# Narrower attention products, a first cumulation of 256 gates, and one operation for the normalisation's small steps

## The chip, the cores and the metric

The kernel runs on one core of a Trainium2 chip. The metric is the device time of one execution in microseconds (us); lower is better. Engines are named as in the profile: PE (TensorE, its weight loads apart as PEld), DVE (VectorE), ACT (ScalarE), POOL (GpSimd), SP (SyncE, which here issues the DMAs).

## The reference

Causal attention with a gate, then two gated feed-forward layers, all in float32. Four batches of eight heads, 576 tokens, head dimension 64; model width 512, hidden width 1536, 2304 tokens.

```python
cum = cumsum(maximum(s, 0), axis=-1)                    # s: 4 x 8 x 576
bias = -(cum[..., :, None] - cum[..., None, :])
scores = where(causal, -1e9, q @ k.T / 8 + minimum(bias, 0))
attn = exp(scores - max(scores)); attn /= sum(attn) + 1e-9
x = (attn @ v)  -> 2304 x 512
xn = x / sqrt(mean(x * x) + 1e-6) * rms_g
x1 = (silu(xn @ w_gate) * (xn @ w_val)) @ w_out
out = (silu(x1 @ w2_gate) * (x1 @ w2_val)) @ w2_out
```

## The kernel before

Every large product is made of three: each operand is split into a high part (type float32r) and a low rest, and high x high, high x low and low x high are summed in PSUM. The instructions are not written in the order in which they run. Each step is recorded with an engine, a planned cost in ns, what it reads and writes, and a priority; `Plan.run` then plays a list schedule and emits every engine's instructions in that fixed order. A step recorded as one operation is emitted in one piece, whatever number of instructions it holds. On the chip each engine works through its list in order and waits where an operand is missing.

**Attention.** Queries are cut into tiles of 128 (the last has 64); group A is tiles 0 and 1 (256 queries), group B tiles 2 to 4 (320). The first 16 units, group A of batches 0 and 1, are *early units* (`EarlyUnit`): true float32 products, loads of 256 keys only. In such a unit the scores of tiles 0 and 1 are products of 128 and 256 columns (L716). The gate's cumulated sum enters as one more row of the contraction: a DMA (L705) copies 256 cumulated gates of this head from `cum` into row 64 of the operand `lq`. DVE adds the mask and takes the least (L601), ACT the exponent with its sum (L612), PE transposes (L726), DVE or ACT copies (L731, L732), PE multiplies by the values (L736), and the result goes to `x` (L741, L742). `cum` itself is made in `setup` by three DVE operations on all 32 heads x 576 gates: clamp (L473), scan (L476), shift and scale (L481).

The other units (`Unit`) take the split form. Group A there appears in batches 2 and 3 only: 16 units. Scores L575: for tile 0, 128 keys are wanted but `max(kl, 256)` columns are multiplied. Values L655: `pT` holds the transposed exponents; windows are padded with zero columns which `clear_pT` writes once, so that key block 1 of group A runs over 256 columns of which 128 are zero, and key block 3 of group B (32 units) over 256 of which 64 are zero. Its last window has 64 columns. Each window is two products, one for each part of `pT`.

**Normalisation** (`normalise`, 8 of them: groups A and B of four batches). ACT squares, PE sums (L767), and then 20 small DVE steps on a tile of 128 x 2 or 3 find each token's factor (L795 to L829). Each is an operation of its own, planned at 70 ns. PE transposes and spreads the factors (L833, L840), DVE multiplies (L844), and the parts of `x` are made (L847, L849).

**First layer's gate and value** (`moe1`, L860): 12 slices of the hidden width, for each group 24 products of 256 or 320 columns a slice. They need the normalised group and that slice's weights. Weights come by DMA (L382) and are converted by ACT, DVE and POOL (L384 to L400). Products of `moe1` have a low priority: PE takes them where attention leaves it free. The output product (L1019) and the second layer follow when attention is over.

Of the kernel before, what the change touches and what calls it, by code (L numbers as in the profile page):

```python
# [9 lines left out]
F32 = mybir.dt.float32  # L10
# [212 lines left out]
def c_mm(n):  # L223
    return 0.4167 * n + 13.3
# [26 lines left out]
TINY = 70  # L251


@with_exitstack
def tile_kernel(
# [87 lines left out]
    pT = {"A": [buf("at", f"pTA{i}", [P, 512], F32R) for i in range(2)],  # L343
# [76 lines left out]

    mask = buf("at", "ft", [P, 2 * P], F32, "mask")

    def setup():
# [44 lines left out]
        def clear_scores(en):  # L468
# [4 lines left out]
        op(DVE, 400, lambda en: en.tensor_scalar(  # L473
            out=cum(), in0=cum(), scalar1=0.0, scalar2=None, op0=ALU.max),
           r=[cum], w=[cum], pri=-1e6)
        op(DVE, 670, lambda en: en.tensor_tensor_scan(  # L476
            cum2(), cum(), cum(), 0.0, op0=ALU.add, op1=ALU.max),
           r=[cum], w=[cum2], pri=-1e6)


        op(DVE, 400, lambda en: en.tensor_scalar(  # L481
            out=cum(), in0=cum2(), scalar1=cum2()[:, S // 2:S // 2 + 1], scalar2=1.0 / SCALE,
            op0=ALU.subtract, op1=ALU.mult), r=[cum2], w=[cum], pri=-1e6)
        op(SP, 4 * NB * NH * S, lambda en: en.dma_start(out=cum_d, in_=cum()),
           r=[cum], w=["cum_d"], pri=-1e6)
# [61 lines left out]
    class Unit:  # L547
# [15 lines left out]
        def scores(self, pri):  # L563
# [53 lines left out]
        def values(self, pri):  # L617
            hd, g, nq = self.head, self.g, self.nq
            j = hd.j
            if g == "A":  # L620
                chunks = [([(1, 1), (0, 0), (0, 1)], [(0, 128, 384, P)])]
                wins = [(0, 256, 256, 0, P, (0,)), (1, 0, 256, 0, P, (0,))]
            else:
# [7 lines left out]
                        (2, 960, 320, 0, P, (1, 2)), (3, 0, 256, 64, P, (0,)),  # L631
# [36 lines left out]
    early_p = [buf("at", f"pTA{i}", [P, 512], F32) for i in range(2)]  # L668
    early_v = [buf("at", f"vl{i}", [P, 5, D], F32) for i in range(2)]

    class EarlyUnit(Unit):
# [6 lines left out]
        def __init__(self, b, h, x, tot):  # L678
# [8 lines left out]
            self.parts = lq_parts(early_q[i % 2], i // 2 % 2)  # L687
            self.vl = early_v[i % 2], i // 2 % 2
# [10 lines left out]
        def load(self, pri):  # L699
# [11 lines left out]
        def scores(self, pri):  # L711
            for t in self.tiles:
# [5 lines left out]
                    start=True, stop=True), r=[*self.parts, "lower rows"], w=[pt], pri=pri)  # L718
# [423 lines left out]
```

## Time and profile before

| | us |
|---|---|
| median of 3 runs | 1151.41 (1149.88 to 1152.21) |
| profiled execution, its own time | 1150.37 |
| its span | 1148.4 |
| PE busy | 1119.2 |
| DVE busy | 607.3 |
| ACT busy | 545.7 |

The span is the time from the first to the last instruction of the profiled execution; 2 us of its own time lie around it. PE is busy for 97% of it, but its busy time counts each product to its modelled end, so a product that follows another closely overlaps it; what a product costs in a row of products is read from the distance of starts. A true float32 product counts as two instructions in the trace. DVE and ACT are busy mostly in the first 300 us, in which attention runs.

### The profile page before, as it was taken

What the parts mean: (1) busy time and instruction counts of PE and PEld (TensorE: products, weight loads), DVE (VectorE), ACT (ScalarE), POOL (GpSimd) and SP (SyncE); (2) the same over time, 40 slices, a digit from 0 to 9 for tenths busy, and PEclk for the clock granted to TensorE, in tenths of its full rate; (3) what the DMA queues carried; (4) which work ended last, traced back from release to release, by engine and by line L of the source; (5) the groups of instructions that cost most, each with busy time, mean ns of one, the idle gap of its engine ahead of it and who ended that gap; (6) DMA issues with size and microseconds to landing.
All of it is one profiled execution on the core that took longest, in us unless ns stands there. A gap on an engine that the chain in (4) does not pass through costs nothing.

```text
span 1148.4 us, 18814 instructions
## 1 busy us (share of the span) xinstructions
PE 1119.2 (97%) x6708; PEld 1001.1 (87%) x6708; DVE 607.3 (53%) x1672; ACT 545.7 (48%) x1203; POOL 188.9 (16%) x282
## 2 busy tenths in 40 slices
PE   5889999999999999999999999999999999999998
PEld 3589999899999999999888788888888888888898
DVE  5898899979735875542686424432222222222222
ACT  5886889889434854431697435432111211211121
POOL 3343455354211300000021000001000100100000
PEclk9899999999999999999999999999999999999999
DMA  4874455334321223338756634211000100100000
GB/s 147 249 239 123 143 142 156 116 104 116 87 72 49 74 89 112 116 119 267 231 163 197 208 122 123 74 37 49 25 1 1 65 1 1 46 1 1 1 37 20
DMA packets 70221, 112.54 MB, mean 98 GB/s; under 512 B 11696, under 2 KB 39344, under 8 KB 70128
## 3 DMA queue, kind: packets, MB, share of 16 engines
q1 hardware_dynamic: 70128, 111.35, 31.6%
q8 instruction: 53, 0.87, 0.3%
q14 instruction: 40, 0.33, 0.1%
HBM read 87.63 MB, written 23.67 MB: 97 GB/s over the span
## 4 chain that ended last, share of the span: by engine, by line
PE 89%; DMA 3%; DVE 3%; ACT 2%; issue 1%; SPq 1%; POOL 0%; DVEq 0%; ACTq 0%
PE mo L860 50%; PE sps L1019 8%; PE tp L1019 8%; PE mo L1019 6%; PE sps L575 4%; PE tp L639 4%; PE tp L655 4%; DMA cvs<-in_w_gv 1%; PE mo L767 1%; PE tp L736 1%; PE sps L716 1%; DVE sc L601 1%; DMA hh<-h_d 1%; DMA lq<-cum 1%; PE tp L726 0%
## 5 line engine op out<-in xcount | busy, mean ns | idle before, releaser
L860 PE MATMUL mo<-xH,H 128*128 128x320 f32 (+1 forms) x768 | 228.1, 298 | 0.1
L860 PE MATMUL mo<-xL,H 128*128 128x320 f32 (+1 forms) x768 | 227.1, 296 | 0.5 <-POOL xL L849 0.5
L860 PE MATMUL mo<-xH,L 128*128 128x320 f32 (+1 forms) x768 | 227.0, 296 | 0.0
L869 DVE SCALAR_TENSOR_TENSOR t<-t,mo 128x256 f32<-128x256 f32 (+2 forms) x156 | 81.3, 521 | 257.7 <-ACT t L867 257.3
L867 ACT ACTIVATE t<-mo 128x256 f32<-128x256 f32 (+2 forms) x156 | 72.2, 463 | 284.8 <-PE mo L860 284.4
L860 PE MATMUL mo<-x1H,L 128*128 128x512 f32 (+1 forms) x480 | 176.6, 368 | 0.0
L860 PE MATMUL mo<-x1H,H 128*128 128x512 f32 (+1 forms) x480 | 176.6, 368 | 0.0
L860 PE MATMUL mo<-x1L,H 128*128 128x512 f32 (+1 forms) x480 | 176.6, 368 | 0.0
L1008 ACT ACTIVATE hH<-hh 128x512 fp32r<-128x512 f32 (+1 forms) x120 | 69.8, 585 | 169.4 <-DVE hh L872 133.1
L860 PEld LDWEIGHTS mo<-xL,H 128*128 128x128 f32 x768 | 144.2, 188 | 1.5 <-POOL xL L849 0.7
L860 PEld LDWEIGHTS mo<-xH,H 128*128 128x128 f32 x768 | 144.1, 188 | 1.0 <-issue 0.3
L860 PEld LDWEIGHTS mo<-xH,L 128*128 128x128 f32 x768 | 144.2, 188 | 0.4
L872 DVE TENSOR_TENSOR hh<-t,mo 128x256 f32<-128x256 f32 (+2 forms) x156 | 81.3, 521 | 99.4 <-PE mo L860 98.1
L1010 DVE TENSOR_TENSOR hL<-hh,hH 128x512 fp32r<-128x512 f32 (+1 forms) x120 | 79.6, 664 | 90.7 <-ACT hH L1008 90.3
L860 PEld LDWEIGHTS mo<-x1L,H 128*128 128x128 f32 x480 | 90.5, 189 | 15.0
L860 PEld LDWEIGHTS mo<-x1H,L 128*128 128x128 f32 x480 | 90.5, 189 | 14.9
L860 PEld LDWEIGHTS mo<-x1H,H 128*128 128x128 f32 x480 | 90.5, 189 | 14.7
L612 ACT ACTIVATE sc<-sc,col 128x512 f32<-128x512 f32 (+4 forms) x160 | 95.6, 598 | 15.6 <-DVE col L601 15.1
L1051 POOL TENSOR_TENSOR x1L<-x1l,x1H 128x512 fp32r<-128x512 f32 (+1 forms) x20 | 25.0, 1260 | 391.5 <-ACT x1H L1049 222.0
L639 PE MATMUL tp<-ident,sc 128*128 128x128 f32 x432 | 69.0, 278 | 1.3 <-DVE x L664 1.1
L1019 PE MATMUL sps<-hL,oH 128*128 128x512 f32 (+1 forms) x192 | 69.6, 364 | 0.1
L1019 PE MATMUL tp<-hL,oH 128*128 128x512 f32 (+1 forms) x192 | 69.4, 363 | 0.0
(129 smaller groups left out, 2097.0 us busy)
## 6 DMA issues: line engine op xcount, KB each, us to landing
raw<-in_w_gv SPq DMA_DIRECT2D x40, 512.0 KB, 4.8
cvs<-in_w_o SPq DMA_DIRECT2D x24, 512.0 KB, 3.7
hh<-h_d SPq DMA_DIRECT2D x48, 256.0 KB, 2.9
cb<-cum_d SPq DMA_DIRECT2D x32, 288.0 KB, 3.4
lq<-in_qk SPq DMA_DIRECT2D x32, 288.0 KB, 3.0
h_d<-hh SPq DMA_DIRECT2D x72, 128.0 KB, 2.2
vl<-in_vp SPq DMA_DIRECT2D x32, 160.0 KB, 3.1
cvs<-in_w_gv SPq DMA_DIRECT2D x8, 512.0 KB, 4.0
```

The costliest lines, as they stand in the source:

```text
L575: op(PE, c_mm(n), lambda en, pt=pt, o=o, c=c, n=n, z=z, kk=kk: en.matmul(pt()[:, :n], qst[j]()[:, o:o + 128], kk()[:, c:c + n], start=z == ...
L612: op(ACT, c_act(o + m, 2) + 35, lambda en: en.activation(sc()[:m, :o + m], sc()[:m, :o + m], ACTF.Exp, scale=-1.0, bias=col()[:m, 0, t:t + 1],
L639: op(PE, C_TR, lambda en, pt=pt, a=a, m=m, kb=kb, t=t: en.transpose(pt()[:, a:a + P], self.sc[t]()[:, kb * P:kb * P + P], ident()), r=[sel ...
L655: op(PE, c_mm(n), lambda en, w=w, z=z, kb=kb, d0=d0, n=n, o=o, kn=kn: en.matmul(po()[:, o:o + n], vst[j]()[:kn, kb, :], pT[g][z]()[:kn, d0 ...
L860: op(PE, c_mm(n), lambda en, a=a, x=x, c=c, k=k, i=i: en.matmul(ps()[:, :n], a()[:, c], x()[:, k, :n], start=(k == 0 and i == 0), stop=(k ...
L867: op(ACT, c_act(n), lambda en: en.activation(t()[:, :n], gp()[:, :n], ACTF.Tanh, scale=0.5), r=[gp], w=[t], pri=pri)
L869: op(DVE, c_tt(n), lambda en: en.scalar_tensor_tensor(out=t()[:, :n], in0=t()[:, :n], scalar=1.0, in1=gp()[:, :n], op0=ALU.add, op1=ALU.mu ...
L872: op(DVE, c_tt(n), lambda en: en.tensor_tensor(out=hh()[:, :n], in0=t()[:, :n], in1=vp_()[:, :n], op=ALU.mult), r=[vp_, t], w=[hh], pri=pri)
L1008: op(ACT, c_act(n) + 35, lambda en: en.activation(H()[:, :n], hh()[:, :n], ACTF.Copy), r=[hh], w=[H], pri=pri)
L1010: op(DVE, c_tt(n), lambda en: en.tensor_tensor(out=L()[:, :n], in0=hh()[:, :n], in1=f32(H()[:, :n]), op=ALU.subtract), r=[hh, H], w=[L], p ...
L1019: op(PE, c_mm(n), lambda en, d=d, c=c, w=w, x=x, i=i: en.matmul(acc_[d]()[:, :n], Wo[w]()[:, c], HL[x]()[:, :n], start=(f == 0 and i == 0) ...
L1051: op(POOL, c_ptt(n), lambda en, k=k, x=x: en.tensor_tensor(out=L()[:, k, :n], in0=x()[:, :n], in1=f32(H()[:, k, :n]), op=ALU.subtract), r= ...
```

## The change

- **Columns.** Scores of tile 0 in group A take 128 columns and not 256; key block 1 of group A takes 128 and not 256, key block 3 of group B 192 and not 256. `clear_pT` goes. The planner's cost of a product, `c_mm`, gets a least value of 72 ns.
- **First group's gates.** `cumulate` makes first a cumulation of 256 gates alone (`cumA`) and then the one of all 576. POOL clears the unused rows of `cumA` first. The first four early units (`FIRST = 4`) don't wait for a DMA of their gates: a second float32 product for each tile adds them, with one column of the identity, spread over 128, as the weights. The other early units copy from `cumA`.
- **Normalisation.** The sum's inverse is one operation of two instructions; the other 18 steps are recorded as one operation, planned at 170 ns each, without the planner's note that it shares a port with POOL.
- **Priorities of weights.** Conversions of `w_gv` come two units later, their loads at 8 + 1.0 f and not 6 + 1.5 f.

```diff
 def c_mm(n):
-    return 0.4167 * n + 13.3
+    return max(72.0, 0.4167 * n + 13.3)
+FIRST = 4
...
+        def clear_cum(en):
+            en.memset(cumA()[NB * NH:64], 0.0)
+            en.memset(cumA()[64:], 0.0)
+        op(POOL, 500, clear_cum, w=[(cumA, 1)], pri=-2e6)
...
+        def cumulate(out, n, pri):
+            rows = NB * NH
+            def steps(en):
+                en.tensor_scalar(out=cum()[:, :n], in0=cum()[:, :n], scalar1=0.0, scalar2=None,
+                                 op0=ALU.max)
+                en.tensor_tensor_scan(cum2()[:, :n], cum()[:, :n], cum()[:, :n], 0.0,
+                                      op0=ALU.add, op1=ALU.max)
+                en.tensor_scalar(out=out()[:rows, :n], in0=cum2()[:, :n],
+                                 scalar1=cum2()[:, n // 2:n // 2 + 1],
+                                 scalar2=1.0 / SCALE, op0=ALU.subtract, op1=ALU.mult)
+            op(DVE, 400 + 3.6 * n, steps, r=[cum], w=[cum, cum2, (out, 0)] if out is not cum
+               else [cum, cum2], pri=pri)
+        cumulate(cumA, 2 * P, -1e6)
+        cumulate(cum, S, -900)
...
-                parts = [(0, max(kl, 256))] if kl <= 512 else [(0, 288), (288, 288)]
+                parts = [(0, kl)] if kl <= 512 else [(0, 288), (288, 288)]
...
-                wins = [(0, 256, 256, 0, P, (0,)), (1, 0, 256, 0, P, (0,))]
+                wins = [(0, 128, 256, 0, P, (0,)), (1, 0, 128, 128, P, (0,))]
...
-                        (2, 960, 320, 0, P, (1, 2)), (3, 0, 256, 64, P, (0,)),
+                        (2, 960, 320, 0, P, (1, 2)), (3, 64, 192, 128, P, (0,)),
...
-            op(SP, 1024, lambda en: en.dma_start(
-                out=ql()[D:D + 1, 1, 288 * i:288 * i + 256], in_=cum()[n:n + 1, 0:256]),
-               r=[cum, "lower rows"], w=self.parts[2:], pri=pri)
+            if not self.first:
+                op(SP, 1024, lambda en: en.dma_start(
+                    out=ql()[D:D + 1, 1, 288 * i:288 * i + 256], in_=cumA()[n:n + 1]),
+                   r=[cumA, "lower rows"], w=self.parts[2:], pri=pri)
...
+                if self.first:
+                    i = self.b * NH + self.h
+                    op(PE, 0.422 * 4 * kl, lambda en, pt=pt, kl=kl: en.matmul(
+                        pt()[:, :kl], ident()[:, i:i + 1].to_broadcast([P, P]), cumA()[:, :kl],
+                        start=False, stop=True), r=[ident, cumA], w=[pt], pri=pri)
...
-            op(DVE, TINY, fn, r=[*w, *r], w=w, pri=pri, port=True)
+            chain.append(fn)
...
+        def factors(en):
+            for fn in chain:
+                fn(en)
+        op(DVE, 170 * len(chain), factors, r=[ps, F], w=[col, fac, rr], pri=pri)
...
-        W1.append(load_gv(w_gv, f, places, tmps1, P_ATT + 10 + 0.5 * f,
-                          P_ATT - 1000 + 6 + 1.5 * f))
+        W1.append(load_gv(w_gv, f, places, tmps1, P_ATT + 12 + 0.5 * f,
+                          P_ATT - 1000 + 8 + 1.0 * f))
-    def clear_pT(en):
...
```

The change moves every engine's order. Three places show how; a line number in the new kernel is about 15 to 33 higher than in the old one.

PE at the program's start, before: `sps` are scores' banks, `lq` an early unit's operands, `tp` transposes and values.

```order
L716 MATMUL sps_165<-lq_101 128x128
L716 MATMUL sps_168<-lq_101 128x256
L716 MATMUL sps_177<-lq_106 128x128
L726 MATMUL tp_181<-ident,sc_170 128x128
L716 MATMUL sps_185<-lq_106 128x256
L726 MATMUL tp_181<-ident,sc_179 128x128 x2
L716 MATMUL sps_201<-lq_101 128x128
L716 MATMUL sps_208<-lq_101 128x256
L736 MATMUL tp_217<-pTA_205,vl_124 64x256
```

And after:

```order
L733 MATMUL sps_149<-lq_116 128x128
L733 MATMUL sps_162<-lq_116 128x256
L739 MATMUL sps_149<-cumA,ident 128x128
L739 MATMUL sps_162<-cumA,ident 128x256
L733 MATMUL sps_176<-lq_121 128x128
L739 MATMUL sps_176<-cumA,ident 128x128
L733 MATMUL sps_182<-lq_121 128x256
L749 MATMUL tp_187<-ident,sc_169 128x128
L739 MATMUL sps_182<-cumA,ident 128x256
L749 MATMUL tp_187<-ident,sc_173 128x128 x2
```

Each product of the first four units is followed by one that adds the gates; the first values of a unit come after those of three units.

DVE in the first normalisation (the chain of the group of batch 0; `rc` and `fac` are its small tiles), before:

```order
L801 TENSOR_REDUCE rc_466<-fac_374 128x2
L389 TENSOR_SCALAR raw_353<-raw_353 128x512
L803 TENSOR_SCALAR rc_466<-rc_466 128x2
L392 SCALAR_TENSOR_TENSOR cvy<-cvy,raw_353 128x512
L805 TENSOR_SCALAR rc_466<-rc_466 128x2
L742 COPY x_114<-tp_470 64x256
L732 COPY pTA_205<-tp_478 128x384
L601 ISA sc_495,col_239<-sps_485,mask 128x128
L601 ISA col_239 128x1
L601 ISA sc_497,col_239<-sps_490,mask 128x256
```

And after:

```order
L765 COPY x_107<-tp_447 64x256
L825 TENSOR_TENSOR fac_383<-mo_301,fac_383 128x16
L826 TENSOR_TENSOR fac_383<-fac_383 128x16
L827 TENSOR_REDUCE rc_461<-fac_383 128x2
L829 TENSOR_SCALAR rc_461<-rc_461 128x2
L831 TENSOR_SCALAR rc_461<-rc_461 128x2
L833 TENSOR_SCALAR rc_461<-rc_461 128x2
L836 SCALAR_TENSOR_TENSOR rc_461<-rc_461 128x2
L838 TENSOR_TENSOR rc_461<-rc_461 128x2
```

Weight conversions and units' steps stood between the chain's steps; now nothing does, through all 18.

PE where `moe1` begins (`mo<-xH,H` and its like; L840 and L873 spread the factors), before:

```order
L840 MATMUL mo_636<-xL_603,sel 128x256
L736 MATMUL tp_631<-pTA_232,vl_127 64x128
L767 MATMUL mo_520<-half,sq_87 128x2 x2
L860 MATMUL mo_649<-xH_633,H_190 128x256
L716 MATMUL sps_651<-lq_106 128x128
L860 MATMUL mo_656<-xH_633,H_190 128x256
```

And after:

```order
L873 MATMUL mo_531<-xL_517,sel 128x256
L733 MATMUL sps_533<-lq_116 128x128
L749 MATMUL tp_520<-ident,sc_504 128x128 x2
L733 MATMUL sps_542<-lq_116 128x256
L893 MATMUL mo_553<-xH_548,H_249 128x256
L893 MATMUL mo_556<-xH_548,H_249 128x256
```

Before, the values of 14 early units stand ahead of the first product of `moe1`; after, those of 11.

## Rows read from the trace of the kernel before

**Rows 1.** The page's head and part 1: busy time, share, instructions.

```profile
span 1148.4 us, 18814 instructions
...
PE 1119.2 (97%) x6708; PEld 1001.1 (87%) x6708; DVE 607.3 (53%) x1672; ACT 545.7 (48%) x1203; POOL 188.9 (16%) x282
```

**Rows 2.** PE's waits: us in total, times, longest; of 0:120, 56:75, 120:300.

```profile
PE sps L716 <- DMA lq<-cum: 13.2, 3, 11.8
...
PE tp L736 <- DVE pTA L732: 2.3, 2, 1.2
...
PE tp L639 <- DVE x L664: 1.1, 1, 1.1
```

**Rows 3.** Busy time by stretch: from:to, length, engines' busy us, granted clock, DMA.

```profile
45.00:50.00 5.00, 3.04 (x11) 1.96 (x11) 4.68 (x21) 4.21 (x11) 1.09 (x1) 0.74 0.95 278
50.00:55.00 5.00, 4.76 (x17) 3.00 (x18) 4.16 (x11) 4.95 (x14) 2.50 (x3) 0.58 0.78 271
...
120.00:300.00 180.00, 177.89 (x1329) 170.18 (x1327) 159.20 (x620) 155.48 (x402) 85.84 (x146) 1.00 0.46 131
```

**Rows 4.** Timeline of the start: start us, duration us, engine, line, operation, idle before it.

```profile
3.19 0.86 DVE L473 TENSOR_SCALAR cum<-cum 32x576 f32<-32x576 f32 x1
4.09 1.35 DVE L476 TENSOR_TENSOR_SCAN cum<-cum 32x576 f32<-32x576 f32 x1
5.47 0.51 DVE L481 TENSOR_SCALAR cum<-cum 32x576 f32<-32x576 f32 x1
5.74 0.39 POOL masks.py:199 TENSOR_SCALAR_AFFINE_SELECT ident<-ident 128x128 f32<-128x128 f32 x1
7.62 2.49 SPq L705 DMA_DIRECT2D lq<-cum  x4
11.36 1.28 ACT L384 ACT_TABLE_LOAD   x1 [11.36 <-DMA raw<-in_w_gv]
11.77 2.08 PE L716 MATMUL sps<-lq 128*128 128x128 f32 x6 [11.77 <-DMA lq<-cum]
12.70 0.29 DVE L601 CUSTOM_DVE_ANT_0 sc<-sps,mask 128x128 f32<-128x128 f32 x1 [6.72 <-PE sps L716]
17.53 1.54 PE L736 MATMUL tp<-pTA,vl 128*64 128x256 f32 x4
```

**Rows 5.** Timeline of PE at early units: scores, values, transposes of one unit each.

```profile
31.32 0.82 PE L716 MATMUL sps<-lq 128*128 128x256 f32 x4
32.12 0.86 PE L736 MATMUL tp<-pTA,vl 128*64 128x256 f32 x4
32.92 0.55 PE L726 MATMUL tp<-ident,sc 128*128 128x128 f32 x3
34.28 0.86 PE L736 MATMUL tp<-pTA,vl 128*64 128x256 f32 x4
```

**Rows 6.** Timeline of the first normalisation: chain's ends on DVE, first product of `moe1`.

```profile
38.10 0.17 DVE L798 TENSOR_TENSOR fac<-mo,fac 128x16 f32<-128x16 f32 x1 [0.29 <-PE mo L767]
50.84 0.17 DVE L829 TENSOR_TENSOR sq<-fac,sq 128x16 f32<-128x16 f32 x1
56.51 0.36 PE L860 MATMUL mo<-xH,H 128*128 128x256 f32 x1
```

**Rows 7.** Timeline of PE, narrow products beside wide ones (a merged row names its first form).

```profile
299.40 1.40 PE L767 MATMUL mo<-half,sq 128*128 128x2 f32 x12
300.66 0.39 PE L860 MATMUL mo<-xH,L 128*128 128x320 f32 x1
...
416.09 0.98 PE L655 MATMUL tp<-pTB,vst 128*128 128x320 f32 x7
...
416.52 0.54 PE L655 MATMUL tp<-pTB,vst 128*128 128x256 f32 x4
...
417.10 0.28 PE L860 MATMUL mo<-xH,L 128*128 128x256 f32 x1
417.22 0.28 PE L860 MATMUL mo<-xH,H 128*128 128x256 f32 x1
```

More of the change, by code (lines that the diff above doesn't have):

```diff
@@ L342, in tile_kernel @@
     vst = [buf("at", f"vst{i}", [P, 5, P], F32R) for i in range(2)]
-    pT = {"A": [buf("at", f"pTA{i}", [P, 512], F32R) for i in range(2)],
+    pT = {"A": [buf("at", f"pTA{i}", [P, 384], F32R) for i in range(2)],
           "B": [buf("at", f"pTB{i}", [P, 1280], F32R) for i in range(2)]}
@@ L419, in tile_kernel @@
     cum = buf("at", "pTB0", [NB * NH, S], F32, "cum")
+    cumA = buf("at", "pTB1", [P, 2 * P], F32, "cumA")
     mask = buf("at", "ft", [P, 2 * P], F32, "mask")
@@ L472, in setup @@
         op([(POOL, 1500), (DVE, 1500)], 0, clear_scores, w=sc4, pri=-1e5)
[L473 to L483, printed above, removed]
+        def cumulate(out, n, pri):
[12 more added lines that the diff above has]
+        cumulate(cum, S, -900)
         op(SP, 4 * NB * NH * S, lambda en: en.dma_start(out=cum_d, in_=cum()),
-           r=[cum], w=["cum_d"], pri=-1e6)
+           r=[cum], w=["cum_d"], pri=-990)
     def lq_parts(b, half):
@@ L666, in values @@
                 op=ALU.add), r=[po, tmp], w=[(x, (hd.h // 2, o))], pri=pri)
-    early_p = [buf("at", f"pTA{i}", [P, 512], F32) for i in range(2)]
+    early_p = [buf("at", f"pTA{i}", [P, 384], F32) for i in range(2)]
     early_v = [buf("at", f"vl{i}", [P, 5, D], F32) for i in range(2)]
@@ L687, in __init__ @@
             self.parts = lq_parts(early_q[i % 2], i // 2 % 2)
+            self.first = i < FIRST
             self.vl = early_v[i % 2], i // 2 % 2
@@ L717, in scores @@
                     pt()[:, :kl], self.qk(0)[:, o:o + P], self.qk(1)[:, :kl],
-                    start=True, stop=True), r=[*self.parts, "lower rows"], w=[pt], pri=pri)
+                    start=True, stop=not self.first), r=[*self.parts, "lower rows"], w=[pt],
+                   pri=pri)
+                if self.first:
[3 more added lines that the diff above has]
+                        start=False, stop=True), r=[ident, cumA], w=[pt], pri=pri)
                 self.least(pt, t, 0, 0, kl, mask, True, True, pri, P - o)
@@ L730, in values @@
             op([(ACT, c_act(384)), (DVE, c_tt(384))], 0, {
-                ACT: lambda en: en.activation(p()[:, 128:], pt()[:, :384], ACTF.Copy),
-                DVE: lambda en: en.tensor_copy(p()[:, 128:], pt()[:, :384])},
+                ACT: lambda en: en.activation(p(), pt()[:, :384], ACTF.Copy),
+                DVE: lambda en: en.tensor_copy(p(), pt()[:, :384])},
                r=[pt], w=[p], pri=pri)
             po = ps_ring("tp", 2)
-            for kb, (o, d0, n) in enumerate(((0, 128, 256), (128, 384, 128))):
+            for kb, (o, d0, n) in enumerate(((0, 0, 256), (128, 256, 128))):
                 op(PE, 0.422 * 4 * n, lambda en, kb=kb, o=o, d0=d0, n=n: en.matmul(
@@ L771, in normalise, with step @@
         fac = ring("m1", "fac", 2, [P, 2, 3, NH], F32)
-        def step(fn, r=(), w=None):
-            w = [col] if w is None else w
-            op(DVE, TINY, fn, r=[*w, *r], w=w, pri=pri, port=True)
+        chain = []
+        def step(fn):
+            chain.append(fn)
         def m():
@@ L827, in columns @@
             return rr().rearrange("p (t h) -> p t h", h=P)[:, :nt, NH * z:NH * z + NH]
[L828 removed]
+        step(lambda en: en.tensor_copy(columns(0).bitcast(F32R), over()))
         step(lambda en: en.tensor_tensor(out=columns(1), in0=over(), in1=columns(0),
[L830 removed]
+                                         op=ALU.subtract))
+        def factors(en):
+            for fn in chain:
+                fn(en)
+        op(DVE, 170 * len(chain), factors, r=[ps, F], w=[col, fac, rr], pri=pri)
         tp = mo_bank()
@@ L939, in tile_kernel @@
     for f in range(KF):
-        W1.append(load_gv(w_gv, f, places, tmps1, P_ATT + 10 + 0.5 * f,
-                          P_ATT - 1000 + 6 + 1.5 * f))
-    def clear_pT(en):
-        for b in pT["B"]:
-            en.memset(f32(b()[:, 0:64]), 0.0)
-        for b in pT["A"]:
-            en.memset(f32(b()[:, 0:128]), 0.0)
-    op([(POOL, 850), (DVE, 850)], 0, clear_pT, w=pT["A"] + pT["B"], pri=P_ATT + len(units))
+        W1.append(load_gv(w_gv, f, places, tmps1, P_ATT + 12 + 0.5 * f,
+                          P_ATT - 1000 + 8 + 1.0 * f))
     moe1([(0, "A", 0), (1, "A", 1)], W1, P_MOE, -1.0e4)
```

23 lines of the change are left out of this document (11 added, 12 removed).

## The prediction, made before the changed kernel ran

> **What bounds the kernel now.** The page's busy times come first: PE is busy for 1119.2 of 1148.4 us [rows 1]. The list of PE's waits says where the rest lies: of what it names in the first 120 us, 13.2 us are one cause, the gates' DMA into the early units, and 11.8 us of that a single wait at the start [rows 2]. From 120 to 300 us PE is busy 177.9 of 180 us [rows 3], and its longest wait there is 1.1 us [rows 2]. So from about 75 us on the time is the sum of PE's products, and before it PE waits. The end moves by what PE loses early, by what its products cost, and by new waits.
>
> Two kinds of loss are seen early. The start: the gates need three DVE operations, 3.19 to 5.98 us, a DMA issued from 7.62 us on, and PE begins at 11.77 [rows 4]. And the stretch before `moe1` has work for PE: the first normalisation's chain begins at 38.10 and ends at 51.01, and `moe1` begins at 56.51 [rows 6]. In the middle of it, 45 to 50 us, PE is busy 3.04 of 5 us, and the granted clock is 0.74, in the next 5 us 0.58, between the levels of 1.2 and 2.4 GHz [rows 3].
>
> **The change part by part.**
>
> *The start.* A DMA and its issue leave the path. 256 of 576 columns of the three operations are between 256/576 of 2.72 us, 1.2 us, and, with a fixed share, some 1.6 us: `cumA` is there at 4.4 to 4.8 us instead of 5.98. The new product also needs the identity, ready at 6.13 us [rows 4] and put back by two new memsets on POOL, at most 0.39 us each if they take as long as its row there: up to 6.9 us, taken as 6.6. At that time DVE is still in the full cumulation, which now stands in its queue ahead of the first L616, to 4.6 + 2.8 = 7.4 us. The first least can start at 7.5 and not at 12.70 us [rows 4], 5.2 us earlier. The table load of ACT, 1.28 us, waited for weights at 11.36 [rows 4]; now it waits for that least, so the first exponent starts near 9.3 us.
> What is added is two products for each of four units, as many columns as the unit's scores: 0.80 us a unit, from the starts at 31.32 and 32.12 [rows 5], about twice that at the start, where four values' products take 1.54 us and later 0.86 [rows 4, 5]. Six of the eight stand in PE's order before the first values, between scores that wait for DVE and ACT anyway. I set 1.2 us of them on the path: the first values at 17.53 - 5.2 + 1.2 = 13.5 us. Bounds: 12.3 (all hidden) to 15.0 (all of the slow ones bare).
>
> *The chain.* The early units then follow at the old pace: 7 of them from 17.53 to 34.28 us, 2.4 each [rows 4, 5]. The eighth unit's values fall at 13.5 + 16.75 + 0.8 (gates of the fourth unit) = 31.0, and the chain follows as before 3.8 us later, at 34.9, since in the new order it waits for one more unit's copy. Its steps measured 0.17 us [rows 6]; 18 in one piece are 3.1 us, to 38.0 us. Before, they took 12.9 us, since conversions and units' steps stood between them. From the chain's end to `moe1` it was 5.5 us [rows 6]: `moe1` begins at 43.5 us and not at 56.51, 13.0 us earlier. What stood between the steps isn't gone: it runs after the chain. On PE that is the difference in the order: 11 units' values ahead of `moe1` and not 14. One unit costs PE 0.80 (scores) + 0.80 (values) + three transposes of 0.11 (the floor found below), 1.9 to 2.0 us [rows 5]: 3 units, 6.0 us, now come behind. So PE has done 13.0 - 6.0 = 7.0 us more of the whole by the same moment.
>
> *Waits behind that.* From 56 to 75 us PE still waits for units: 2.3 us in two waits for a copy on DVE [rows 2], about 1.1 us for each unit left. Five units are left now, not two or three: 2.5 us more, between 0 (products of `moe1` cover them) and 5 us.
>
> *Columns.* 64 products of 256 columns get 128 (16 units, scores and values, two parts each), and 64 of 256 get 192 (32 units, two parts). A product of 256 columns costs 0.118 us, one of 320 costs 0.143 [rows 7]. What a narrow one costs is seen twice. Twelve products of 2 columns take 1.26 us from the first's start to the next other one's: 0.105 us each. And from 416.52 to 417.10 two of 256, two of 64 and one of 256 take 0.58 us: 0.58 - 3 x 0.118 leaves 0.226, 0.113 for each of 64 columns [rows 7]. So a product doesn't fall below some 0.11 us, and one of 128 or 192 columns gains 0.008: 128 x 0.008 = 1.0 us. Bounds: 0, and 4.8 us if columns alone counted (64 columns are then 0.143 - 0.118 = 0.025: 64 x 0.050 + 64 x 0.025 = 4.8).
> The same floor is what the Trainium skill's page "TensorE: Matmul & The Clock Gate", section "LDWEIGHTS (loading the stationary operand)", would make of it: a load takes the weights' 128 columns at 1.2 per ns, 107 ns, whatever the moving columns are; the trace agrees, with 0.11 for 2 and for 64 columns.
>
> *Nothing, or little.* `clear_pT` goes: four memsets on DVE, not on the path. The 256-column copies into `pTA` stay as large. DMAs of the gates of 12 later units only change their source. The weights' later conversions hurt only if `moe1` runs out of weights: that is in the rivals.
>
> *Later normalisations.* Seven more chains hold DVE for 3.1 us in one piece. From 120 to 300 us DVE is busy 159.2 of 180 us and ACT 155.5 [rows 3], so what queues behind a chain (least, rests of `pT`, results to `x`) comes late by up to 3 us, and PE waits for it unless products of `moe1` stand between. Against that: the plan now counts these steps at 170 ns, near the measured 0.17, not at 70, so the orders should fit better. I take 0, bounds -2 (the waits there, 1.1 us and smaller, go) and the rival's price.
>
> Sum: -13.0 + 6.0 + 2.5 - 1.0 = -5.5 us. The profiled execution's own time, 1150.4, lies 1.0 below the median of 1151.4, and the comparison is made with medians: 1151.4 - 5.5 = 1145.9. Its own range is 1142 to 1149: start and chain 2.5 us less or 1.5 more, waits 2.5 either way, not all at once.
>
> **The rivals.** What a measurement of this kernel can tell from no change is about 0.2%, 2.3 us: below 1149.1 is faster, above 1153.7 slower.
>
> *Columns count in full.* For it: from 320 to 256 columns the cost does fall with the columns, 0.143 to 0.118. Against it: the pair of 64 columns at 0.226 us [rows 7]. Price 3.8 us more: 1142.1. On the Trainium skill's page "TensorE: Matmul & The Clock Gate", section "Back-to-back issue gap", a product of 128 columns takes 134 cycles, 56 ns; by that the time would be 1140.6, an estimate, and the pair at 0.226 us does not agree with it.
>
> *The lead is given back.* PE gets ahead, but what limits the next 200 us are ACT and DVE, 86% and 88% busy there [rows 3]; or `moe1`, 13 us earlier, outruns the weights, whose conversions come two units later. Then PE's lead shrinks to what ACT and DVE gain themselves: ACT begins its work at about 8 and not at 11.36 us [rows 4] but has the same list; with 1.4 us more on DVE (the second cumulation) I keep 2 us, with the columns 3: 1148.4; and if all is given back but the columns, 1150.4. For it: the high shares. Against it: PE has no wait over 1.1 us there, so `moe1` has cover left.
>
> *Slower: the chain holds DVE.* Six chains fall in 100 to 475 us. Each stops, for 3.1 us, the least and the copies which PE's next attention products wait for. If PE's order has no products of `moe1` at these places, PE stands for up to 3.1 less one least of 0.3 [rows 4], 2.8 us each: 6 x 2.8 = 16.8, less the 5.5: 1162.7. It passes no change at 0.9 us a chain and slower begins at 1.3 us a chain. For it: DVE is 88% busy. Against it: no wait of PE there was over 1.1 us [rows 2], though chains and conversions stood in the same queue, and `moe1` has the lowest priority and is spread through the order.
>
> **How the numbers follow.** Forecast 0.55 (1142 to 1149), columns in full 0.09, lead given back 0.25 (0.13 of it at about 1148.4, 0.12 near 1150.4), chain holds DVE 0.11 (0.08 above 1153.7, 0.03 within). Faster: 0.55 + 0.09 + 0.13 = 0.77; same: 0.12 + 0.03 = 0.15; slower 0.08. Left out of the range are the upper 0.11 and about 0.07 at the lower end: 1141 to 1151.
>
> **What would show it.** First product on PE near 5 to 7 us and first least near 7.5; the first chain's 18 rows in 3.1 us and `moe1` from about 43 us; no granted clock below 1 after that; distance of starts of products with 128 and 192 columns at 0.11 us; PE's waits in 43 to 75 us about 5 us. It is wrong if PE waits after 75 us for DVE behind a chain (L837 to L855), or for weights, or if the first chain begins after 38 us.

## The result and the profile of the changed kernel

The changed kernel takes 1164.12 us (median; 1163.41 to 1172.58) beside 1151.34 us of the kernel before on the same chip: a ratio of 1.0130, 95% interval 1.0107 to 1.0153 (ratios here are estimated from the runs of both kernels together; that of the medians alone is 1.0111). It is slower by 13 us where 5.5 us faster was forecast.

The page of its profiled execution (1163.41 us), span and busy times; before these were 1148.4 and 1119.2 [rows 1]:

```profile
span 1161.6 us, 18879 instructions
PE 1126.1 (97%) x6724; PEld 1007.7 (87%) x6724; DVE 618.8 (53%) x1661; ACT 546.3 (47%) x1204; POOL 199.9 (17%) x293
```

The span grew by 13.2 us: 6.9 us of that are PE's busy time, and 6.3 us its idle time (span less busy: 29.2 before, 35.5 now). Two things have to be explained, waits and slower products.

The start of the changed kernel in the timelines of PE, DVE and ACT (start us, duration us, what it is, and in brackets the idle time before it and what ended it), to be laid beside [rows 4] and [rows 6]:

```profile
0.72 1.28 ACT L627 ACT_TABLE_LOAD   x1 [0.72 <-PEq L1159]
4.62 1.62 PE L733 MATMUL sps<-lq 128*128 128x128 f32 x4 [4.62 <-DMA lq<-in_qk]
7.81 0.29 DVE L616 CUSTOM_DVE_ANT_0 sc<-sps,mask 128x128 f32<-128x128 f32 x1 [0.44 <-PE sps L739]
8.14 0.40 ACT L627 ACTIVATE sc<-sc,col 128x128 f32<-128x128 f32 x1 [6.14 <-DVE col L616]
12.97 0.43 PE L759 MATMUL tp<-pTA,vl 128*64 128x256 f32 x1
33.71 0.17 DVE L825 TENSOR_TENSOR fac<-mo,fac 128x16 f32<-128x16 f32 x1
33.92 0.17 DVE L826 TENSOR_TENSOR fac<-fac 128x16 f32<-128x16 f32 x1
...
37.20 0.17 DVE L855 TENSOR_TENSOR sq<-fac,sq 128x16 f32<-128x16 f32 x1
40.92 0.35 PE L893 MATMUL mo<-xH,H 128*128 128x256 f32 x1 [0.65 <-ACT xH L880]
```

The first least comes at 7.81 us (12.70 before), the first values at 12.97 (17.53), the first chain ends at 37.37 and `moe1` begins at 40.92 and not at 56.51. The first least is 0.3 us later than forecast, the rest earlier. The loss is later. PE's list of waits (us in all, times, longest us):

```profile
PE mo L866 <- DVE sq L855: 17.7, 7, 5.1
```

L866 is the pair or three of transposes behind a normalisation's chain, L855 the chain's last step. An eighth such wait of 0.9 us is listed under a DMA; with it they are 18.6 us. This wait is new in size: before, no wait after 120 us was over 1.1 us [rows 2]. From 120 to 300 us PE's busy time went from 177.9 us [rows 3] to 176.0, and the granted clock there from 1.00 to 0.99:

```profile
120.00:300.00 180.00, 175.98 (x1289) 168.22 (x1288) 153.26 (x580) 148.77 (x382) 86.05 (x146) 0.99 0.44 126
```

**One such wait, on three engines.** The timelines of PE, DVE and POOL around the sixth chain, 311 to 319 us:

```profile
313.34 0.31 PE L893 MATMUL mo<-xH,L 128*128 128x320 f32 x1
318.30 0.85 PE L866 MATMUL mo<-ident,sq 128*128 128x128 f32 x3 [4.65 <-DVE sq L855]
319.21 0.47 PE L893 MATMUL mo<-xL,H 128*128 128x320 f32 x1
319.48 0.47 PE L893 MATMUL mo<-xH,L 128*128 128x320 f32 x1
...
311.72 0.73 DVE L829 TENSOR_SCALAR rc<-rc 128x3 f32<-128x3 f32 x1
312.48 0.81 DVE L831 TENSOR_SCALAR rc<-rc 128x3 int32<-128x3 int32 x1
313.52 0.16 DVE L836 SCALAR_TENSOR_TENSOR rc<-rc 128x3 f32<-128x3 f32 x1
313.72 1.31 DVE L838 TENSOR_TENSOR rc<-rc 128x3 f32<-128x3 f32 x1
...
315.26 1.25 DVE L836 SCALAR_TENSOR_TENSOR rc<-rc 128x3 f32<-128x3 f32 x1
318.06 0.18 DVE L855 TENSOR_TENSOR sq<-fac,sq 128x24 f32<-128x24 f32 x1
...
311.69 0.73 POOL L882 TENSOR_TENSOR xL<-x,xH 128x256 fp32r<-128x256 f32 x1 [0.90 <-ACT xH L880]
312.38 0.87 POOL L556 TENSOR_TENSOR vst<-vl,vst 128x320 fp32r<-128x320 f32 x1
313.61 1.40 POOL L547 TENSOR_TENSOR kLL<-lq,kHH 128x576 fp32r<-128x576 f32 x1 [0.36 <-ACT kHH L540]
315.08 1.40 POOL L544 TENSOR_TENSOR qst<-lq,qst 64x576 fp32r<-64x576 f32 x1
```

Three things are to be seen. The chain took 7.2 us, and not 3.1: a step alone lasts 0.16 to 0.18 us, with starts 0.20 apart, but each of the four long steps shown begins while an operation of POOL runs and ends with that one (0.73, 0.81, 1.31, 1.25 beside 0.73, 0.87, 1.40, 1.40). PE had products for 2.5 us of it and then stood 4.65 us. And the products behind the wait start 0.27 us apart (319.21 to 319.48) where those of the same form start 0.147 apart otherwise: the clock had fallen. The windows around the third chain say so directly (PE busy us, granted clock):

```profile
165.00:170.00 5.00, 3.12 (x24) 1.00 0.75 215
170.00:175.00 5.00, 4.23 (x20) 0.66 0.16 56
175.00:180.00 5.00, 5.00 (x43) 1.00 0.12 33
```

The wait of 2.66 us that ended at 170.77 is followed by products at 1.2 GHz; then it is 2.4 GHz again.

**Where the 13 us came from, along the work.** PE does the same products in every one of these kernels but for a few columns and the eight new products of the gates. So one can ask at what time each kernel has done as much of them as the kernel before at a given time. Each product is counted as its starts are apart at full clock (0.113 us up to 192 columns, 0.120 for 256, 0.147 for 320; the gates' eight new ones as nothing), summed in PE's order, and the times at the same sum are compared. The table gives, in us, how late each kernel is (negative: early); it is right to about 1 us.

```
time     changed  a_steps  a_first  a_pieces  a_bank  a_port  a_bank_port  b_chain  b_gates  b_cols  a_steps200
  35      -5.1     -5.0     -4.6     -4.7     -5.0    -4.6     -5.5         -0.7     -4.9     -0.5     -4.8
  75     -13.4     -7.8    -13.4    -12.8    -12.7   -12.3    -13.3         -5.5     -8.3     -1.1     -4.3
 105      -5.1     -5.1     -3.5     -3.3     -6.1    -6.3      1.2          2.6     -4.6     -1.1      5.5
 160      -5.1     -5.0     -3.7     -3.7     -6.0    -6.1      1.4          3.7     -5.0     -1.1      5.3
 310       1.1     -6.2     -5.0     -4.2      8.3     7.8      4.0         16.4     -4.7     -2.1      3.3
 450      11.6     -7.8     -6.5     -3.1     12.3    19.6      7.9         19.9     -4.7     -3.9      3.4
```

At 160 us the changed kernel was 5.1 us ahead; the forecast's sum was 5.5. From 160 to 450 us, where six chains lie, it lost 16.6 us. The columns behind the first are the experiments. By the spans the changed kernel ends 13.2 us late, 1.6 more than at 450 us; what happens behind 450 us was not looked into.

### The profile page after: what moved, and what is told of

Read it like the earlier page. It is cut to its first block, busy times and chain, and to the rows that moved or that the text cites. A ratio compares the mean times of both kernels' runs of the same rounds, so it can differ in the third digit from the quotient of the medians.

```text
span 1161.6 us, 18879 instructions
## 1 busy us (share of the span) xinstructions
PE 1126.1 (97%) x6724; PEld 1007.7 (87%) x6724; DVE 618.8 (53%) x1661; ACT 546.3 (47%) x1204; POOL 199.9 (17%) x293
## 4 chain that ended last, share of the span: by engine, by line
PE 66%; DVE 3%; ACT 3%; DMA 1%; issue 1%; DVEq 0%; ACTq 0%
PE mo L893 41%; PE sps L1046 8%; PE tp L1046 8%; PE mo L1046 3%; PE tp L670 1%; PE tp L654 1%; DMA hh<-h_d 1%; PE sps L590 1%; ACT hH L1035 1%; DVE hL L1037 1%; ACT cvy L386 1%; PE mo L790 0%; ACT cvy L388 0%; DVE cvy L394 0%; ACT oo L1055 0%
## 5 line engine op out<-in xcount | busy, mean ns | idle before, releaser
L1078 POOL TENSOR_TENSOR x1L<-x1l,x1H 128x512 fp32r<-128x512 f32 (+1 forms) x20 | 25.7, 1296 | 418.7 <-ACT x1H L1076 329.3
L1046 PE MATMUL tp<-hH,oL 128*128 128x512 f32 (+1 forms) x192 | 69.5, 363 | 0.0
```

The lines of the kernel that those rows point to most:

```text
L1046: op(PE, c_mm(n), lambda en, d=d, c=c, w=w, x=x, i=i: en.matmul(acc_[d]()[:, :n], Wo[w]()[:, c], HL[x]()[:, :n], start=(f == 0 and i == 0) ...
L1078: op(POOL, c_ptt(n), lambda en, k=k, x=x: en.tensor_tensor(out=L()[:, k, :n], in0=x()[:, :n], in1=f32(H()[:, k, :n]), op=ALU.subtract), r= ...
```

## The experiments

Theory 1 was that the chain in one piece is the loss, and theory 2 that it is the rest: `moe1` so early that the weights come late, or the weights' priorities. First the chain alone, taken away and put in.

**a_steps**, the changed kernel with the steps as operations of their own:

```diff
-        def step(fn):
-            chain.append(fn)
...
-        op(DVE, 170 * len(chain), factors, r=[ps, F], w=[col, fac, rr], pri=pri)
+        def step(fn, r=(), w=None):
+            w = [col] if w is None else w
+            op(DVE, TINY, fn, r=[*w, *r], w=w, pri=pri, port=True)
```

> The changed kernel with one part undone: the 20 small steps of the normalisation are operations of their own again, planned at 70 ns each, as in the kernel before; the start, the columns and the weights' priorities stay changed. Theory 1 (the chain in one piece is the whole loss): PE's waits before the normalisation's transposes, 18.6 us in the changed kernel (8 of them, 0.5 to 5.1 us), fall below 1 us each, the chains lie between other work of DVE again, and the time is the kernel before's less what the start and the columns give, 1144 to 1149 us. Theory 2 (the loss is in the other parts: `moe1` so early that weights and conversions come late, or the weights' priorities): the time stays at 1160 to 1165 us. If the loss is shared, it lies between, near 1155.

Measured: 1144.27 us, ratio to before 0.9936 (0.9915 to 0.9957), the fastest of all that ran. Its page and its waits at the transposes (now L856):

```profile
PE 1119.0 (98%) x6724; PEld 1001.3 (88%) x6724; DVE 605.9 (53%) x1665; ACT 544.5 (48%) x1203; POOL 199.6 (18%) x290
...
PE mo L856 <- DVE sq L852: 1.7, 2, 1.5
```

The same 6724 products keep PE busy for 1119.0 and not 1126.1 us, and its idle time is 21.0 and not 35.5 us: of the 21.6 us between the two spans 14.5 are idle time of PE and 7.1 are products that took longer at a lower clock. Its chains (the same 18 steps, L823 to L852) last 3.7 to 18.3 us, six of the eight longer than any in the changed kernel, and PE hardly notices: products of `moe1` go on beside them.

**b_chain**, the kernel before with the chain in one piece alone (the same lines the other way round).

> The kernel before with that one part alone: the normalisation's 18 steps behind the reciprocal as one operation of DVE, planned at 170 ns a step. Theory 1 (the chain in one piece is the loss): PE waits 10 to 20 us before the transposes in all and the time is 1160 to 1170 us; the first chain still gives a few us of the 13 that the forecast saw in it. Theory 2 (other parts): 1149 to 1153 us. The forecast itself would have had -4 us here, 1147.

Measured: 1169.41 us, 1.0148 (1.0121 to 1.0176). The -4 us that I ascribe to the forecast there was wrong by 22 us; -4.5 is its term for start and chain together, and the chain's own share of it is smaller, as worked out below. From 160 to 450 us it lost 16.2 us, as the changed kernel did. Theory 1 holds; theory 2 falls.

Then why PE stands. Three reasons were possible: the sums' PSUM bank, which the one operation holds to the chain's end, so that only three of four are left for `moe1`'s gates and values (1a); DVE's queue, where the `hidden` steps that empty those banks and the least and copies for the attention stand behind the chain (1b); and POOL, which stretches the chain (1c).

**a_bank**:

```diff
-        step(lambda en: en.tensor_tensor(out=u(), in0=squares(), in1=over(), op=ALU.mult))
+        op(DVE, 170, lambda en: en.tensor_tensor(out=u(), in0=squares(), in1=over(), op=ALU.mult),
+           r=[ps, F], w=[(fac, 1)], pri=pri)
...
-        op(DVE, 170 * len(chain), factors, r=[ps, F], w=[col, fac, rr], pri=pri)
+        op(DVE, 170 * len(chain), factors, r=[F], w=[col, fac, rr], pri=pri)
```

> The changed kernel with one line moved: the first step of the chain, which alone reads the sums of the squares in PSUM, is an operation of its own, and the 17 others stay one operation, which no longer names the sums' bank. DVE is held as long as before (17 of 18 steps), but the bank comes free some 3 us earlier. Theory 1a (PE stands because the bank is held, so that `moe1` has no two banks for its next gate and value): PE's products of `moe1` go on during the chain, the waits before the transposes fall from 18.6 us to below 6 us, and the time is 1148 to 1154 us. Theory 1b (PE stands because DVE's queue is held: least, copies and `hidden` come late): the waits stay above 12 us in all, some under other names, and the time is within 3 us of 1164.

Measured: 1163.20 us, 1.0099 (1.0080 to 1.0117): neither. Page, waits, and PE behind the sixth chain (its 17 steps run from 308.82 to 312.26 us, with nothing from POOL) and a window behind the fifth (291.89 to 297.61, stretched by POOL):

```profile
PE 1132.9 (98%) x6724; PEld 1015.1 (87%) x6724; DVE 620.8 (53%) x1667; ACT 545.1 (47%) x1205; POOL 190.9 (16%) x286
...
PE mo L867 <- DVE t L903: 5.6, 2, 3.6
PE mo L867 <- DVE sq L856: 5.4, 2, 2.9
...
313.64 0.49 PE L867 MATMUL mo<-ident,sq 128*128 128x128 f32 x3
...
300.00:305.00 5.00, 5.00 (x25) 0.50 0.54 172
```

The idle time did fall, to 28.5 us. PE waits 1.9 to 3.6 us at the four chains that POOL stretched to 5.3 to 7.1 us, and not at the four of 3.4 to 3.5 us (313.64 has no wait). Half of what is left is now a wait for `hidden`'s step L903, behind the chain in DVE's queue: 1a and 1b are both there, one behind the other. But PE is busy for 6.8 us more than in the changed kernel with the same products: behind the wait of 2.49 us that ended at 297.76 the clock was 0.50 in the whole of the next window. What the waits gave, the clock took.

**a_port**:

```diff
-        op(DVE, 170 * len(chain), factors, r=[ps, F], w=[col, fac, rr], pri=pri)
+        op(DVE, 203 * len(chain), factors, r=[ps, F], w=[col, fac, rr], pri=pri, port=True)
```

> The changed kernel with the chain planned at 203 ns a step, which is what it takes alone (3.66 us for 18), and with the note that keeps the plan from putting POOL's large operations beside it, as the separate steps had it. The bank is held as in the changed kernel. Theory 1c (the chains are long because POOL works beside them: 5.3, 4.9, 7.3 and 7.2 us where three others took 3.7, together 9.9 us more): most chains take 3.7 us, PE's waits fall by 6 to 10 us, the time is 1154 to 1158 us. If what is decisive is that PE has nothing to do for the length of the chain whatever it is: waits of 2.5 to 3.5 us at six chains remain, 15 us or more, and the time is above 1160 us.

Measured: 1171.29 us, 1.0168 (1.0144 to 1.0191), the slowest. (One of its four executions took 3430 us, for a reason that nothing here shows; the other three took 1169.72 to 1172.30, and the ratio is theirs.) Five of its eight chains take 3.66 us, without POOL; three are still stretched, since the chip's times are not the plan's. Page, waits, and PE beside the fifth chain, which ran from 289.90 to 293.56 with nothing from POOL:

```profile
PE 1138.7 (97%) x6724; PEld 1018.1 (87%) x6724; DVE 616.4 (53%) x1658; ACT 546.5 (47%) x1206; POOL 200.2 (17%) x294
...
PE mo L866 <- DVE sq L855: 13.2, 6, 3.7
...
293.62 0.69 PE L866 MATMUL mo<-ident,sq 128*128 128x128 f32 x2 [2.67 <-DVE sq L855]
```

So an unstretched chain can leave PE without work when the bank is held: 2.67 us here, 2.83 and 1.84 at the seventh and eighth, though nothing at the first and sixth. The waits at the transposes did fall by 5.4 us, from 18.6 to 13.2, a little less than 1c's 6 to 10, and yet the time rose. The clock shows why. PE from 160 to 450 us in the changed kernel, in a_bank and in a_port (length, PE busy, granted clock):

```profile
160.00:450.00 290.00, 276.92 (x2009) 0.98 0.33 95
160.00:450.00 290.00, 280.56 (x2000) 0.95 0.33 95
160.00:450.00 290.00, 278.51 (x1950) 0.94 0.32 94
```

PE stands 13.1 us in the changed kernel, 9.4 in a_bank and 11.5 in a_port (2.6 in the kernel before), but the clock's shortfall from 1.00 is 0.02, 0.05 and 0.06 of 290 us, some 6, 15 and 17 us. Each of the two edits cut the waiting and lost more by the clock than it saved. 1c alone doesn't give the time; why the clock stayed low for longer there is open.

**a_bank_port**, both edits at once.

> The changed kernel with both edits at once: the chain's first step alone, so that the sums' bank comes free, and the other 17 planned at 203 ns a step with the note that keeps POOL's large operations away. With the bank edit alone PE waited only at the four chains that POOL had stretched (4.4 to 6.1 us; waits of 1.9 to 3.6), and 0 to 0.4 us at those of 3.2 us. Theory A (PE has 2.3 to 3.2 us of work beside a chain when the bank is free, so a chain that POOL leaves alone costs nothing): the waits at the transposes fall below 4 us in all, the granted clock stays above 0.99, the time is 1146 to 1152 us. Theory B (an operation of 3 us on DVE starves PE whatever else is done): waits of 8 us or more, clock below 0.99, 1158 us or more.

Measured: 1160.55 us, 1.0098 (1.0083 to 1.0113). By the total, theory B; by the place, mostly A: from 160 to 450 us it lost 6.6 us, where the changed kernel lost 16.6, the bank edit 18.3 and the POOL edit 25.7. Each edit alone gains nothing there and both together 10 us. The total is spoilt elsewhere, by one chain, the second: POOL worked beside it for 6.1 of its 8.0 us, and PE stood 7.05 us:

```profile
PE mo L867 <- DVE t L903: 7.0, 1, 7.0
...
77.34 1.52 DVE L839 TENSOR_TENSOR rc<-rc 128x2 f32<-128x2 f32 x1
...
77.45 1.39 POOL L547 TENSOR_TENSOR kLL<-lq,kHH 128x576 fp32r<-128x576 f32 x1
```

**a_pieces** cuts the chain in three:

```diff
-        op(DVE, 170 * len(chain), factors, r=[ps, F], w=[col, fac, rr], pri=pri)
+        for k in range(0, len(chain), 6):
+            def factors(en, k=k):
+                for fn in chain[k:k + 6]:
+                    fn(en)
+            op(DVE, 203 * 6, factors, r=[ps, F] if k == 0 else [col, F],
+               w=[col, fac] if k < 12 else [col, fac, rr], pri=pri, port=True)
```

> The changed kernel with the chain in three operations of 6 steps (1.2 us each, planned at 203 ns a step, POOL's large operations kept away), only the first of which reads the sums' bank. Theory A (what costs is how long DVE's queue and the bank are held in one go): from 160 to 450 us the kernel loses nothing against the one with separate steps (that of separate steps loses -1.5 us there against the kernel before, the changed one 17.8, the bank edit with the POOL edit 7.6), waits at the transposes below 3 us in all, 1144 to 1149 us. Theory B (any chain that the plan sees as a block of DVE starves PE): 8 us or more lost there, 1152 us or more.

Measured: 1150.17 us, 0.9996 (0.9984 to 1.0009), just above theory A's range, with one wait at the transposes left, 2.5 us at 77 us. From 160 to 450 us it lost 0.6 us against the kernel before, with a clock of 1.00 and no wait over 0.5 us there. Theory A had compared with a_steps, which gains 2.8 there (the expectation's own figures differ from the table's by 1.1 to 1.3 us, about what the table is right to): against that a_pieces lost 3.4 us, not nothing, in a stretch in which no wait shows it. So three pieces give back 16 of the 19.4 us that lie between the changed kernel and a_steps in this stretch: what costs is mostly how long DVE and the bank are held in one go. Of the kernels with POOL's note, a_port lost 25.7 us, a_bank_port with the bank freed early 6.6, and a_pieces with DVE freed as well 0.6; the note and the price of the step alone are not the cure, but bank and queue are told apart by these orders only roughly, since each edit makes a new plan. What else a_pieces lacks to a_steps it lost at 75 to 105 us, where its lead of 5.0 us became 1.8 behind.

Next the forecast's own terms.

**a_first**, the chain in one piece at the first normalisation only:

```diff
+        fused = not once
+        once.append(1)
...
+            if fused and r != [tot] and chain is not None and (chain or ps in r):
+                chain.append(fn)
+                return
```

> The changed kernel with the chain in one piece at the first normalisation only; the seven later ones in separate steps. This is the forecast's term for the chain by itself, against the run with all steps separate (1144.3 us, `moe1` from 48.4 us, first chain 33.2 to 43.0). The forecast's working, with these starts: `moe1` 7.5 us earlier, less the units moved behind (two of 2.0 us) and the waits behind them: 1 to 3 us faster, 1141 to 1143. The rival (the lead is given back in 43 to 75 us, where DVE and ACT have the same list): within 2 us of 1144.3, with as much more of PE's waits before 75 us as `moe1` is earlier.

Measured: 1145.19 us, 0.9962 (0.9950 to 0.9975): the rival, within a us of a_steps. `moe1` begins at 40.93 and the kernel is 5.6 us ahead of a_steps at 75 us; at 105 us it is 1.6 behind. So the lead was given back, but at 75 to 105 us and not, as the rival had it, before 75. Its waits and its windows (PE, PEld, DVE, ACT, POOL busy, clock):

```profile
PE mo L898 <- ACT H L398: 3.8, 4, 1.7
...
85.00:90.00 5.00, 2.09 (x7) 1.04 (x5) 4.52 (x12) 1.26 (x2) 3.88 (x5) 0.77 0.51 142
90.00:95.00 5.00, 4.63 (x23) 4.63 (x24) 3.21 (x10) 3.41 (x9) 1.55 (x3) 0.55 0.57 202
```

L398 converts the weights of `moe1`: PE had reached products whose weights weren't there, and then ran at the lower clock.

**b_gates**, the kernel before with the first group's gates alone; the core of its diff:

```diff
+            self.first = i < FIRST
...
+                if self.first:
+                    i = self.b * NH + self.h
+                    op(PE, 0.422 * 4 * kl, lambda en, pt=pt, kl=kl: en.matmul(
+                        pt()[:, :kl], ident()[:, i:i + 1].to_broadcast([P, P]), cumA()[:, :kl],
+                        start=False, stop=True), r=[ident, cumA], w=[pt], pri=pri)
```

> The kernel before with the first group's gates alone (the partial cumulation and the two more products of the first four units); steps, columns and priorities as before. The forecast's term for the start: first values 4 us earlier, so 1147 to 1148 us, if nothing gives it back. The rival: the stretch before 60 us is limited by ACT and DVE, whose lists are no shorter, and the gain shrinks to 2 us or less: 1149.5 to 1151.5.

Measured: 1145.28 us, 0.9968 (0.9955 to 0.9980). It is 4.9 us ahead at 35 us and 4.7 at 450: the start's term was right, and it is kept (by the medians 4.4 us, more than the 3 to 4 expected).

**b_cols**, the kernel before with the fewer columns alone:

```diff
-                parts = [(0, max(kl, 256))] if kl <= 512 else [(0, 288), (288, 288)]
+                parts = [(0, kl)] if kl <= 512 else [(0, 288), (288, 288)]
...
-                wins = [(0, 256, 256, 0, P, (0,)), (1, 0, 256, 0, P, (0,))]
+                wins = [(0, 128, 256, 0, P, (0,)), (1, 0, 128, 128, P, (0,))]
```

> The kernel before with the fewer columns alone (the products of 128 and 192 columns, the smaller `pTA`, `clear_pT` gone, and the plan's price of a narrow product). The forecast: 1.0 us less, 1150.4, which this measurement can't tell from no change; columns counted in full, 4.8 us less, 1146.6. A move of over 3 us either way with the narrow products' starts still 0.11 us apart would be the new order in the plan and not the columns.

Measured: 1147.62 us, 0.9983 (0.9972 to 0.9994). More than 1.0 us, and not all of it columns: from 45 to 55 us, where the clock had been 0.74 and 0.58 [rows 3], it is now 1.00, though PE is busy there for no longer. From 160 to 450 us, where most narrow products are, it gains 2.8 us more; how much of that is their cost is worked out below.

```profile
45.00:50.00 5.00, 2.29 (x12) 1.00 0.89 256
50.00:55.00 5.00, 4.66 (x24) 1.00 0.85 251
```

**a_steps200** and **a_steps_noprio** change a number each in a_steps: `op(DVE, TINY, fn` to `op(DVE, 200, fn`, and the weights' priorities back to `P_ATT + 10 + 0.5 * f` and `P_ATT - 1000 + 6 + 1.5 * f`.

> The changed kernel with separate steps, planned at 200 ns each, as the trace has them, and not at 70. If a truthful duration makes a better order, the time falls below 1144.3 us (1140 to 1143); if the plan now spends DVE's time on a chain of 20 x 200 = 4 us whose real steps lie between other work anyway, and so puts the chains later or PE's products of `moe1` in front of them too early, it is 1146 us or more. I hold 1143 to 1146 for likeliest: no difference.

> The changed kernel with separate steps and, besides, the weights' priorities of the kernel before (conversions two units earlier). If the priorities matter by themselves, the stretch from 60 to 105 us, where `moe1` waits for conversions of weights, moves by 2 us or more either way: below 1142 or above 1146.5 us. If conversions there are limited by what ACT, DVE and POOL can do in all, whatever their order, 1142.5 to 1146.

Measured: 1154.90 us, 1.0037 (1.0019 to 1.0055), and 1145.88 us, 0.9956 (0.9939 to 0.9974). The priorities make no difference that can be measured. The 200 ns do, against my expectation: with the duration that the trace shows the order is 10 us worse. All of it is lost before 105 us (5.5 us late there, a_steps 5.1 early), 3.8 us of it in one wait for a weights' conversion, and part of the rest by the clock (0.89 from 45 to 105 us, 0.97 in a_steps); from 160 to 450 us it loses nothing. So the stretch from 45 to 105 us is moved by up to 10 us by how the plan's order falls there, with the chain in pieces or not. Why this order is bad and not that one isn't settled by these runs; they show what PE waited for.

## Why the prediction was wrong, by its steps

**The start: right.** First values at 12.97 us and not 17.53 (forecast 13.5), first least at 7.81 (7.5). The exponent came at 8.14 and not 9.3: the table load didn't wait for the least as I had put it, it ran at 0.72. b_gates keeps 4.4 us of it by the medians.

**The chain: its moments right, its worth given back.** The chain ended at 37.37 (38.0) and `moe1` began at 40.92 (43.5). Its steps start 0.20 us apart and not 0.17: I took the duration of a step for the distance of two, so 3.66 us and not 3.1. The term was -13.0 + 6.0 + 2.5 = -4.5 us for start and chain together: 3.2 of the 13.0 us are the start (the chain begins at 34.9 and not at 38.10), so the chain's own share is 13.0 - 3.2 - 6.0 - 2.5 = 1.3 us. At 75 us the one piece is worth 5.6 us (changed kernel against a_steps), more than that; at 105 us nothing. In the changed kernel the second chain took it (7.3 us long, PE stood 5.1 us), and in a_first, where that chain is in steps, the weights' conversions took it. What failed here is that I closed the account at 75 us. That the changed kernel is 5.1 us ahead at 160 us, near the sum of 5.5, is luck: a_steps and b_gates are 5.0 us ahead there without the one piece, by the start. The rival "the lead is given back" had this cause in a half-sentence: `moe1` outruns the weights.

**Columns: right.** In the changed kernel a pair of score products of 128 columns takes 0.17 us to the next product, the first 0.06 and the second 0.11 (254.88, 254.94, 255.05). But the wide product behind the pair then takes 0.20 us to the next one (255.05 to 255.25) and not the 0.147 of its form:

```profile
254.88 0.22 PE L590 MATMUL sps<-kHH,qst 128*128 128x128 f32 x1
254.94 0.28 PE L590 MATMUL sps<-kLL,qst 128*128 128x128 f32 x1
255.05 0.36 PE L893 MATMUL mo<-xL,H 128*128 128x320 f32 x1
255.25 0.31 PE L893 MATMUL mo<-xH,L 128*128 128x320 f32 x1
255.39 0.31 PE L893 MATMUL mo<-xH,H 128*128 128x320 f32 x1
```

With that delay the pair costs 0.17 + 0.05 = 0.22 us, 0.11 for each, as the forecast's floor had it, beside 0.236 for two of 256. The 32 pairs of 128 (16 of scores, 16 of values) so save 0.013 us each; at the 32 windows of 192 it is 0.362 and not 0.377 us from the first of the two to the product behind the two of 64. That is 0.9 us in all, where 1.0 was forecast. b_cols measured 2.4 us by the medians (its interval is 0.7 to 3.2). What goes beyond the columns there belongs, as far as the trace shows it, to the new order: the clock at 45 to 55 us, and PE standing 1.4 and not 2.6 us between 160 and 450.

**Later normalisations: this step failed.** It was put at 0 and cost 16.6 us. Two arguments carried the 0. One was that no wait of PE there was over 1.1 us although chains and conversions stood in the same queue [rows 2]. But the chains were not in the queue in one piece then: in a_steps they last up to 18.3 us and PE's longest wait behind one is 1.5 us, since what empties PE's banks stands between their steps. The low waits were the merit of what the change took away. The other was that the plan counts the steps nearly as long as they are. They took 3.66 us alone, and 4.9 to 7.3 in four of eight chains, beside POOL: the change had dropped the note that keeps POOL's large operations away, which stands in the diff and which I didn't cost.

**The rival "the chain holds DVE"** had the right side, and its 1162.7 is near the 1164.12; its mechanism was half right. It let PE wait for the least and the copies behind the chain, 2.8 us at each of six. What PE waits for is the chain itself, at its own transposes: the six waits are 2.66, 1.08, 0.53, 4.65, 2.83 and 0.91 us, 12.7 in all. With the kernel before's own 2.6 us of standing set off, 10 us of the 16.6 are waits, and the other 6 or so are the clock behind them (0.98 of 290 us), which the rival didn't price. That its number came so near is therefore in part luck. I gave it 0.11 because I weighed DVE's share of busy time against `moe1`'s low priority. What should have been counted is what PE can do from the sums to the transposes with the banks it has: a bank takes the 12 products of one gate or value, 1.8 us at 0.147 each, and the chain was 3.1 by my own sum. In the changed kernel 6 to 19 products of `moe1` and at some chains a few of attention started beside the six chains.

## What to carry to other kernels

Before small steps are joined to one operation, find what stands between them now, and add up what the waiting engine can still do, with the buffers that the joined operation holds, until its result is due; the share of busy time doesn't say that. A lead won early is worth only what the next limit leaves of it, so the sum must go on to the place where the order runs into its next supply, here the converted weights. And a wait of some us on TensorE is paid again in the products behind it.

## What the runs showed of the hardware

The clock. PE's waits of 2.49 to 7.05 us at joined chains were each followed within 5 us by products at 0.50, 1.2 GHz, for some us (0.66 in the window 170 to 175 of the changed kernel, 0.50 in all of 300 to 305 in a_bank). Of the shorter ones some were (1.91 us in a_bank, 2.02 in b_chain) and some not (2.15 us in b_chain, ended 443.50). The clock also fell where no wait was longer than 0.61 us: in a_bank_port that wait and 18 products of 2 columns lie between 420.7 and 424.5 us, the granted clock is 0.84 from 420 to 425, and in the window behind it 0.50 with PE busy all the time. In a_steps 18 products of 2 columns without a wait in front (from 295.95 and from 297.87 us) lie in a window that stays at 1.00. The rows of a_bank_port, then that of a_steps:

```profile
421.35 1.50 PE L790 MATMUL mo<-half,sq 128*128 128x2 f32 x12 [0.61 <-ACT sq L784]
...
425.00:430.00 5.00, 5.00 (x26) 0.50 0.02 5
...
295.00:300.00 5.00, 5.00 (x40) 1.00 0.22 79
```

DVE and POOL. A DVE step of 0.16 us lasts 1.31 us when an operation of POOL with 576 elements is running, and ends with it. The Trainium skill's page "SBUF — State Buffer", section "Who interferes with whom", says that a DVE instruction with two inputs in SBUF contends with one of GpSimd that reads SBUF. The rows at 313.72 and 315.26 us agree. The steps at 311.72 and 312.48, with one input each, were held too; that sentence doesn't cover them. Not every operation of POOL does this: beside the mask's affine select (L604 of the changed kernel, 0.55 us for two from 316.56 us, which reads `cb` in SBUF) the steps at 316.74 and 316.94, also with two inputs, kept 0.16 and 0.19 us. There the trace does not agree, and why is open.
